# First MLP products begun before attention step 3 joins, first weight loads in halves, all weights loaded ahead of step 4

## The chip, the cores and the metric

The kernel runs on one core of a Trainium2 chip. The metric is the device time of one execution in microseconds (us). Executions more than 1.5% above the fastest of the same kernel are called slow and are left out of all comparisons. Each changed kernel ran beside the kernel before, on the same chip in the same rounds. Two changed kernels of different sets are compared by their medians, which is rougher. A ratio is the mean time of one kernel's fast runs over the mean of the other's of the same rounds, with a 95% interval, so it is not quite the ratio of the medians that stand beside it.

Engines in the profiles: PE multiplies matrices (PEld loads its weights), DVE, ACT and POOL are the vector, scalar and general engines, SP issues DMAs.

## The reference

A decayed linear attention in blocks of 64 tokens, then an MLP on its output:

```python
for b in range(12):                              # per batch and head
    intra = (qb @ kb.T * Dmask) @ vb
    inter = (qb * lam_pow) @ kv_state
    out[:, :, sl] = intra + inter
    kv_state = lam_block * kv_state + (kb * rev_pow).T @ vb
x = attention output as 3072 tokens x 512
return gelu_tanh(x @ w_in) @ w_out               # 512 -> 2048 -> 512
```

Inputs and output are float32; the kernel multiplies in float16 with float32 sums. q, k and v are 4 x 8 x 768 x 64, w_in and w_out are 4 MB each.

## The kernel before

The work is cut into 24 attention *steps* (256 tokens and half of the heads each). For one step: `load_step` (three DMAs of 256 KB), `prep` (scale and cast q, k, v), `stage_t` (transposes on PE, a copy to `qkT`), scores (`Sps`), causal mask (`PT`), products into two output banks (`OK`), a state update (`t` on DVE, `u` on POOL), and a copy into `xT`. Steps make *groups*: group 0 is steps 0 to 3 and has 512 tokens. When a group is in `xT`, its MLP is queued as *filler*: 16 products f (`mm1`: four matmuls of 512 columns and one gelu on ACT), then the second matrix product in parts of four matmuls (`mm2`). The schedule draws filler between the pieces of later steps. Some names that come up again: wi0 to wi3 and wo0 to wo3 are the 1 MB pieces of w_in and w_out; f counts the 16 blocks of 128 columns of w_in, c the four blocks of 128 rows that a product sums over; a *bank* is one of the six PSUM buffers of `ps_M`; t_2_1 is the `t` of `U(2)`.

```python
    pin(nc.sync.dma_start(out=lam_bc[:], in_=lam.unsqueeze(0).to_broadcast([P, H])))
    for s in range(4):
        load_step(s)
    for j in range(4):
        load_win(j)
    load_wout(0)
    load_wout(1)
    load_step(4)
    load_wout(2)
    load_wout(3)
    load_step(5)
    ...
    def cast_wout(j):                       # float32 piece j of w_out to float16
        for i in range(2):
            ...
            if i == 1 and j >= 2:
                pin(nc.scalar.activation(out=dst, in_=src, func=AF.Copy))
            else:
                pin(nc.gpsimd.tensor_copy(out=dst, in_=src))
    ...
        def mm1(f0):                        # one bank of the six in ps_M
            Hps = ps_M.tile([P, per, N], FP32, tag="M", name="Hps")
            ...                             # four matmuls
            pin(nc.scalar.activation(out=gT[:, f0 : f0 + per, :], in_=Hps[:],
                                     func=AF.Gelu_apprx_tanh))
    ...
    idle(12)                                # the head: steps 0 to 3
    prep(0)
    ...
    stage_t(3)
    idle(3)
    R(3, 2, split=True)
    idle(3)
    R(None, 3)                              # step 3 into xT; group 0 queued
    cast_win(0)
    U(2)                                    # t and u of the second block
    U(3)

    for j in range(1, 4):
        cast_win(j)
    for j in range(2):
        cast_wout(j)
    fill(17)                                # all 16 products and one mm2 part
    prep(4)
    cast_wout(2)
    cast_wout(3)
    stage_t(4)
    fill(3)
    R(4, None)
```

`pin` keeps instructions in program order on each engine. So `cast_wout(2)` stands on ACT behind all gelus of group 0.

## Time and profile before

| | before |
|---|---|
| median of 4 runs | 214.70 us (214.63 to 214.76) |
| span of the profiled execution | 213.5 us |
| PE busy | 205.1 us |
| last matmul's copy starts (end of PE's path) | 209.93 us |

The profiled execution took 215.29 us, 0.6 us above this median and outside the four runs. So a difference of up to some 0.6 us between this profile and another can be the execution's and not the kernel's.

### The profile page before, as it was taken

The numbers are of one execution on the slowest core, as the hardware profiler recorded it, in microseconds if no ns is written. First come the engines' busy times: TensorE is split into PE (matmuls) and PEld (weight loads), VectorE is DVE, ScalarE is ACT, GpSimd is POOL, SyncE is SP. The second block draws the span as 40 slices with busy tenths as digits, with TensorE's granted clock in tenths as the row PEclk, the third lists the DMA queues.
The fourth block names the chain that finished last, engine by engine and source line by source line (L and its number), as shares of the span: only waits on it lengthen the run. The fifth ranks groups of instructions, "written<-read, shape, count | busy, mean of one in ns | idle before, by whom it ended". The sixth has DMA issues, their size and how long they took to land.

```text
span 213.5 us, 5059 instructions
## 1 busy us (share of the span) xinstructions
PE 205.1 (96%) x2118; PEld 107.0 (50%) x2118; DVE 91.3 (43%) x179; ACT 94.2 (44%) x175; POOL 64.2 (30%) x82
## 2 busy tenths in 40 slices
PE   7879999999999999999999999999999999999993
PEld 2444444455875784444455455444455454444452
DVE  4887522478784523740464541363632241100121
ACT  2375774342672471477420577420576211475000
POOL 5493136454582333422421320432420110000000
PEclk9999999999999999999999999999999999999999
DMA  5999999999999999893675673615120012100112
GB/s 135 301 331 391 383 352 370 286 288 325 303 221 223 309 208 253 221 227 71 176 211 144 205 194 69 180 53 150 49 52 0 0 52 98 54 0 0 49 63 86
DMA packets 61879, 37.82 MB, mean 177 GB/s; under 512 B 17696, under 2 KB 54816, under 8 KB 61856
## 3 DMA queue, kind: packets, MB, share of 16 engines
q1 hardware_dynamic: 61696, 37.37, 63.4%
q8 instruction: 16, 0.26, 0.5%
q10 hardware_dynamic: 160, 0.13, 0.2%
q14 instruction: 7, 0.06, 0.1%
HBM read 27.27 MB, written 6.29 MB: 157 GB/s over the span
## 4 chain that ended last, share of the span: by engine, by line
PE 86%; DMA 7%; SPq 2%; ACT 2%; DVE 1%; issue 0%; ACTq 0%
PE Hps L376 38%; PE O2ps L387 34%; DMA k<-in_k_dram 7%; PE Sps L257 3%; PE OK L316 3%; PE OK L306 3%; SPq L67 2%; PE O2ps L407 2%; PE Tps L219 1%; PE OK L270 1%; ACT qkT L223 1%; ACT xT L324 1%; ACT qk L200 1%; DVE PT L291 0%; PE idle L432 0%
## 5 line engine op out<-in xcount | busy, mean ns | idle before, releaser
L376 PE MATMUL Hps<-xT,w_in 128*128 128x512 f16 (+1 forms) x448 | 86.0, 349 | 0.3 <-ACT xT L324 0.3
L387 PE MATMUL O2ps<-w_out,gT 128*128 128x512 f16 x368 | 82.9, 379 | 0.0
L378 ACT ACTIVATE gT<-Hps 128x512 f16<-128x512 f32 x96 | 57.3, 596 | 34.5 <-PE Hps L376 33.7
L376 PEld LDWEIGHTS <-w_in 128*128 128x128 f16 x448 | 43.3, 98 | 38.1 <-issue 0.6
L351 POOL TENSOR_TENSOR u<-t,lumask 128x256 f16<-128x256 f32 x40 | 27.9, 706 | 91.1 <-DVE t L347 64.2
L387 PEld LDWEIGHTS <-gT 128*128 128x128 f16 x368 | 35.3, 98 | 39.7
L291 DVE TENSOR_TENSOR PT<-Sps,mask 128x1024 f16<-128x1024 f32 (+1 forms) x25 | 29.4, 1180 | 45.2 <-PE Sps L257 45.2
L324 ACT ACTIVATE xT<-OK 128x256 f16<-128x256 f32 x48 | 18.3, 451 | 51.3 <-PE OK L316 39.5
L394 DVE COPY o<-O2ps 128x512 f32<-128x512 f32 x23 | 15.8, 690 | 52.6 <-PE O2ps L387 52.5
L201 POOL TENSOR_TENSOR v<-v,dv 128x512 f16<-128x512 f32 x24 | 25.9, 1081 | 4.7 <-DMA v<-in_v_dram 4.6
L195 DVE TENSOR_TENSOR qk<-q,dq 128x512 f16<-128x512 f32 x23 | 19.7, 859 | 6.9 <-DMA q<-in_q_dram 6.9
L200 ACT ACTIVATE qk<-k 128x512 f16<-128x512 f32 x24 | 15.0, 623 | 9.3 <-DMA k<-in_k_dram 9.3
L347 DVE SCALAR_TENSOR_TENSOR t<-t,lamu,OK 128x64 f32<-128x64 f32 x64 | 14.5, 274 | 2.4 <-PE OK L270 1.4
L432 PE MATMUL idle<-ones 128*128 128x512 f16 x30 | 10.2, 479 | 1.5 <-DVE ones L126 1.5
L257 PEld LDWEIGHTS <-qkT 64*64 64x64 f16 x384 | 6.1, 106 | 10.1 <-issue 6.8
L257 PE MATMUL Sps<-qkT 64*64 64x128 f16 x384 | 10.0, 222 | 0.9 <-ACT qkT L223 0.7
L103 POOL CAST w_out<-wo 128x1024 f16<-128x1024 f32 x6 | 6.6, 1113 | 12.4 <-DMA wo<-in_moe_w_out_dram 12.4
L306 PE MATMUL OK<-PT,v 64*64 64x128 f16 x384 | 10.2, 218 | 0.0
L316 PE MATMUL OK<-qkT,u 128*128 128x128 f16 x80 | 8.6, 222 | 0.0
L219 PE MATMUL Tps<-ident,qk 128*128 128x128 f16 x72 | 6.1, 221 | 2.2 <-DVE qk L195 1.0
L306 PEld LDWEIGHTS <-v 64*64 64x64 f16 x384 | 6.8, 108 | 0.9 <-issue 0.8
L219 PEld LDWEIGHTS <-qk 128*128 128x128 f16 x72 | 4.6, 99 | 5.0 <-DVE qk L195 1.8
(34 smaller groups left out, 54.4 us busy)
## 6 DMA issues: line engine op xcount, KB each, us to landing
q<-in_q_dram SPq DMA_DIRECT2D x24, 256.0 KB, 4.7
k<-in_k_dram SPq DMA_DIRECT2D x24, 256.0 KB, 4.9
v<-in_v_dram SPq DMA_DIRECT2D x24, 256.0 KB, 5.2
out_dram<-o SPq DMA_DIRECT2D x23, 256.0 KB, 2.7
wi<-in_moe_w_in_dram SPq DMA_DIRECT2D x4, 1024.0 KB, 11.4
wo<-in_moe_w_out_dram SPq DMA_DIRECT2D x4, 1024.0 KB, 9.4
qkT<-qk SPq DMA_TRANSPOSE x15, 3.4
out_dram<-o SPq DMA_DIRECT2D x1, 96.0 KB, 2.2
```

The source lines that it names most:

```text
L195: pin(q_eng.tensor_tensor(wide(tq), q32[:], decay(dq), ALU.mult))
L200: pin(nc.scalar.activation(out=wide(tk), in_=k32[:], func=AF.Copy))
L201: pin(nc.gpsimd.tensor_tensor(wide(tv[:]), v32[:], decay(dv), ALU.mult))
L257: pin(nc.tensor.matmul(Sps[half64(c), hl, hp, jk, :], o[half64(hl), 1, jk, hp, half64(c)], o[half64(hl), 0, :, hp, half64(c)], start=True, ...
L291: pin(nc.vector.tensor_tensor(dst.rearrange("p a c d -> p a (c d)"), src.rearrange("p a c d -> p a (c d)"), mask[:].unsqueeze(1).to_broadc ...
L306: pin(nc.tensor.matmul(OK[c][half64(hl), hp * P : hp * P + P], tv[half64(c), jk, 2 * hp + hl, :], PT[hp][half64(c), hl, jk, :], start=star ...
L324: pin(nc.scalar.activation(out=dst[:, :, c * P : (c + 1) * P].rearrange("p hp (t j) -> p hp j t", j=2), in_=OK[c][:, 0:256].rearrange("p ( ...
L351: pin(nc.gpsimd.tensor_tensor(bd[:], t[:].unsqueeze(2).to_broadcast([P, 2, 2, D]), lumask[:, 2 * half : 2 * half + 2, :].unsqueeze(3).to_b ...
L376: pin(nc.tensor.matmul(Hps[:, i, :], w_in16[:, c, f * P : (f + 1) * P], x[:, c, :], start=(c == 0), stop=(c == NC - 1)))
L378: pin(nc.scalar.activation(out=gT[:, f0 : f0 + per, :], in_=Hps[:], func=AF.Gelu_apprx_tanh))
L387: pin(nc.tensor.matmul(O2[tau][:], gT[:, f, tau * P : (tau + 1) * P], w_out16[:, f, :], start=(f == 0), stop=(f == NF - 1)))
L394: pin(nc.vector.tensor_copy(out=o32[:], in_=o2[:]))
```

## The change

The intent: the head spends 30 idle matmuls and several waits before the MLP can start. If products f=0 to 3 of group 0 begin with what is there (c=0,1 on all 512 columns, c=2,3 on the first 256, without step 3's heads and tokens) and step 3 joins later, PE has useful work sooner. For that the first w_in tiles must come sooner, hence the loads in halves, and the weights go ahead of step 4 in the queue of loads. Some smaller things are moved along with it. The core of the diff (cut: helpers that were split, and that DVE in place of ACT now copies step 3's `qkT`):

```diff
-    wst = ctx.enter_context(tc.tile_pool(name="wst", bufs=4))
+    wst = ctx.enter_context(tc.tile_pool(name="wst", bufs=6))
...
-    pin(nc.sync.dma_start(out=lam_bc[:], in_=lam.unsqueeze(0).to_broadcast([P, H])))
+    pin(nc.scalar.dma_start(out=lam_bc[:], in_=lam.unsqueeze(0).to_broadcast([P, H])))
     for s in range(4):
         load_step(s)
     for j in range(4):
-        load_win(j)
-    load_wout(0)
-    load_wout(1)
-    load_step(4)
-    load_wout(2)
-    load_wout(3)
-    load_step(5)
-    for s in range(6, 9):
+        load_win(j, 2 if j < 2 else 1)
+    for j in range(4):
+        load_wout(j)
+    for s in range(4, 9):
         load_step(s)
...
+        def mm1_begin(f):
+            first[f] = ps_M.tile([P, N], FP32, tag="M", name="Hps")
+            for c in range(NC):
+                w = N if c < 2 else SB
+                pin(nc.tensor.matmul(first[f][:, 0:w], ...))
+        def mm1_end(f):
+            for c in range(2, NC):
+                pin(nc.tensor.matmul(first[f][:, SB:N], ...))
+            pin(nc.scalar.activation(out=gT[:, f, :], in_=first.pop(f)[:],
+                                     func=AF.Gelu_apprx_tanh))
...
-    idle(12)
+    idle(11)
...
-    prep(3)
-    R(2, 1)
-    stage_t(3)
-    idle(3)
-    R(3, 2, split=True)
-    idle(3)
-    R(None, 3)
-    cast_win(0)
+    products(None, 2)
+    cast_win(0, 0, 128, 128)
+    cast_win(0, 128, 512, 128, on_act=True)
+    scores(3)
+    queue_group(0)
+    fill(1)
+    products(3, None)
+    update(3, 0)
+    causal(3)
+    fill(2)
+    products(None, 3)
+    fill(5)
+    cast_win(1, 0, 512, 128)
     U(2)
     U(3)

-    for j in range(1, 4):
+    for j in range(2, 4):
         cast_win(j)
-    for j in range(2):
+    for j in range(3):
         cast_wout(j)
-    fill(17)
+    fill(21)
+    cast_wout(3)
     prep(4)
-    cast_wout(2)
-    cast_wout(3)
     stage_t(4)
-    fill(3)
+    prep(5)
+    fill(2)
     R(4, None)
     U(4)
-    prep(5)
-    fill(4)
+    fill(1)
     stage_t(5)
     prep(6)
-    fill(2)
+    fill(1)
     R(5, 4)
```

More of the change, by code (lines that the diff above doesn't have):

```diff
@@ L74, with load_win @@
     wstage = {}
-    def load_win(j):
+    def load_win(j, halves=1):
+        w = 512 // halves
         t = wst.tile([P, NC, 512], FP32, tag="w32", name=f"wi32_{j}")
-        pin(nc.sync.dma_start(out=t[:], in_=moe_w_in[:, j * 512 : (j + 1) * 512].rearrange(
-            "(c p) f -> p c f", p=P)))
+        src = moe_w_in[:, j * 512 : (j + 1) * 512].rearrange("(c p) f -> p c f", p=P)
+        for i in range(0, 512, w):
+            pin(nc.sync.dma_start(out=t[:, :, i : i + w], in_=src[:, :, i : i + w]))
         wstage[("i", j)] = t
@@ L86, in load_wout, with cast_win @@
         wstage[("o", j)] = t
-    def cast_win(j):
-        t = wstage.pop(("i", j))
-        w = 128 if j == 0 else 256
-        for i in range(0, 512, w):
-            pin(nc.vector.tensor_copy(out=w_in16[:, :, j * 512 + i : j * 512 + i + w],
-                                      in_=t[:, :, i : i + w]))
+    def cast_win(j, lo=0, hi=512, w=256, on_act=False):
+        t = wstage[("i", j)]
+        for i in range(lo, hi, w):
+            dst = w_in16[:, :, j * 512 + i : j * 512 + i + w]
+            src = t[:, :, i : i + w]
+            if on_act:
+                pin(nc.scalar.activation(out=dst, in_=src, func=AF.Copy))
+            else:
+                pin(nc.vector.tensor_copy(out=dst, in_=src))
     def cast_wout(j):
@@ L180, in prep, with wide, decay, prep_v @@
     def prep(s):
-        half = s % 2
-        q32, k32, v32 = ld32.pop(s)
-        hs = slice(half * HH, (half + 1) * HH)
-        def wide(t):
-            return t.rearrange("p j h d -> p h j d")
-        def decay(t):
-            return t[:, hs, :].unsqueeze(3).to_broadcast([P, HH, 2, D])
+        prep_qk(s)
+        prep_v(s)
+    def wide(t):
+        return t.rearrange("p j h d -> p h j d")
+    def decay(t, s):
+        hs = halves[s % 2]
+        return t[:, hs, :].unsqueeze(3).to_broadcast([P, HH, 2, D])
+    def prep_v(s):
+        tv = a16p.tile([P, 2, HH, D], FP16, tag="v16", name=f"v16_{s}")
+        pin(nc.gpsimd.tensor_tensor(wide(tv[:]), ld32[s][2][:], decay(dv, s), ALU.mult))
+        a16[s] = a16[s] + (tv,)
+        if s >= 6:
+            load_ahead(s + 3)
+    def prep_qk(s):
+        q32, k32, _ = ld32[s]
         tqk = a16p.tile([P, 2, 2, HH, D], FP16, tag="qk16", name=f"qk16_{s}")
         tq, tk = tqk[:, 0], tqk[:, 1]
-        tv = a16p.tile([P, 2, HH, D], FP16, tag="v16", name=f"v16_{s}")
         q_eng = nc.gpsimd if s == 3 else nc.vector
-        pin(q_eng.tensor_tensor(wide(tq), q32[:], decay(dq), ALU.mult))
+        pin(q_eng.tensor_tensor(wide(tq), q32[:], decay(dq, s), ALU.mult))
         if s == 0:
@@ L200, in prep @@
         pin(nc.scalar.activation(out=wide(tk), in_=k32[:], func=AF.Copy))
-        pin(nc.gpsimd.tensor_tensor(wide(tv[:]), v32[:], decay(dv), ALU.mult))
-        a16[s] = (tq, tk, tv)
+        a16[s] = (tq, tk)
         if s >= FIRST_DMA_T:
@@ L207, in prep @@
             qkT[s] = o
-        if s >= 6:
-            load_ahead(s + 3)
     def stage_t(s):
@@ L213, in stage_t @@
             return
-        tq, tk, _ = a16[s]
+        tq, tk = a16[s][:2]
         Tps = ps_M.tile([P, 2, 2, 2, P], FP16, tag="M", name="Tps")
@@ L221, in stage_t @@
         o = qkp.tile([P, 2, 2, 2, P], FP16, tag="qkT", name=f"qkT_{s}")
-        if 1 <= s <= 3:
+        if 1 <= s <= 2:
             pin(nc.scalar.activation(out=o[:], in_=Tps[:], func=AF.Copy))
@@ L235, in half64, with scores, causal, products @@
         return slice(64 * i, 64 * i + 64)
-    def region(n, s, split=False):
+    Ss = {}
+    def scores(n):
+        o = qkT[n]
+        Sps = ps_S.tile([P, 2, 2, 2, P], FP32, tag="S", name="Sps")
+        for hp in range(2):
+            for jk in range(2):
+                for hl, c in TILES:
+                    pin(nc.tensor.matmul(
+                        Sps[half64(c), hl, hp, jk, :], o[half64(hl), 1, jk, hp, half64(c)],
+                        o[half64(hl), 0, :, hp, half64(c)], start=True, stop=True,
+                        skip_group_check=True))
+        Ss[n] = Sps
+    def causal(n):
+        t = ptp.tile([P, 2, 2, 2, P], FP16, tag="PT", name=f"PT_{n}")
+        pin(nc.vector.tensor_tensor(
+            t[:].rearrange("p a b c d -> p (a b) (c d)"),
+            Ss.pop(n)[:].rearrange("p a b c d -> p (a b) (c d)"),
+            mask[:].unsqueeze(1).to_broadcast([P, 4, 2 * P]), ALU.mult))
+        PTs[n] = t
+    def products(n, s):
         OK = [ps_M.tile([P, 512], FP32, tag="M", name=f"OK{c}") for c in range(2)]
@@ L248, in region @@
         if n is not None:
-            o = qkT[n]
             _, tk, tv = a16[n]
-            Sps = ps_S.tile([P, 2, 2, 2, P], FP32, tag="S", name="Sps")
-            def scores():
+            last = (n // 2) % NSB == NSB - 1
+            for jk in range(2):
                 for hp in range(2):
-                    for jk in range(2):
-                        for hl, c in TILES:
-                            pin(nc.tensor.matmul(
-                                Sps[half64(c), hl, hp, jk, :],
-                                o[half64(hl), 1, jk, hp, half64(c)],
-                                o[half64(hl), 0, :, hp, half64(c)], start=True, stop=True,
-                                skip_group_check=True))
@@ L263, in products @@
-            def products():
-                last = (n // 2) % NSB == NSB - 1
-                for jk in range(2):
-                    for hp in range(2):
-                        for c, hl in TILES:
-                            if c == 1 and last:
-                                continue
-                            pin(nc.tensor.matmul(
-                                OK[c][half64(hl), 256 + hp * D : 256 + hp * D + D],
-                                tk[half64(c), jk, 2 * hp + hl, :],
-                                tv[half64(c), jk, 2 * hp + hl, :],
-                                start=start(c, hl), stop=(jk == 1), skip_group_check=True))
-                Kps[n] = OK
@@ L277, in region @@
-            if split:
-                products()
-                update(n, 0)
-                scores()
-            else:
-                scores()
-                products()
-            PT = []
-            for hps in ([slice(0, 1), slice(1, 2)] if split else [slice(0, 2)]):
-                w = hps.stop - hps.start
-                t = ptp.tile([P, 2, w, 2, P], FP16, tag=f"PT{w}", name=f"PT_{n}_{hps.start}")
-                for src, dst in ([(Sps[:, :, hps.start], t[:, :, 0])] if split else
-                                 [(Sps[:].rearrange("p a b c d -> p (a b) c d"),
-                                   t[:].rearrange("p a b c d -> p (a b) c d"))]):
-                    pin(nc.vector.tensor_tensor(
-                        dst.rearrange("p a c d -> p a (c d)"),
-                        src.rearrange("p a c d -> p a (c d)"),
-                        mask[:].unsqueeze(1).to_broadcast([P, 2 * w, 2 * P]), ALU.mult))
-                PT += [t[:, :, i] for i in range(w)]
@@ L296, in region @@
-            PTs[n] = PT
+                    for c, hl in TILES:
+                        if c == 1 and last:
+                            continue
+                        pin(nc.tensor.matmul(
+                            OK[c][half64(hl), 256 + hp * D : 256 + hp * D + D],
+                            tk[half64(c), jk, 2 * hp + hl, :], tv[half64(c), jk, 2 * hp + hl, :],
+                            start=start(c, hl), stop=(jk == 1), skip_group_check=True))
+            Kps[n] = OK
         if s is None:
@@ L307, in region @@
                         OK[c][half64(hl), hp * P : hp * P + P], tv[half64(c), jk, 2 * hp + hl, :],
-                        PT[hp][half64(c), hl, jk, :], start=start(c, hl), stop=False,
+                        PT[half64(c), hl, hp, jk, :], start=start(c, hl), stop=False,
                         skip_group_check=True))
-        ins = ins_of.pop(s)
         for c in range(2):
-            u = ins[c]
-            if u is None:
+            if c == 0 and sbg % NSB == 0:
                 continue
+            u = us.pop((s, 0) if c else (s - 2, 1))
             for hp in range(2):
@@ L327, in region, with update @@
                 func=AF.Copy))
-    ins_of = {}
-    def update(s, c):
+    us = {}
+    def update(s, c, parts="tu"):
         sbg, half = divmod(s, 2)
         sb = sbg % NSB
-        if c == 0:
-            ins_of[s] = [state[half][1] if sb > 0 else None, None]
         if c == 1 and sb == NSB - 1:
@@ L339, in update @@
             return
-        OK = Kps[s] if c == 0 else Kps.pop(s)
-        K = OK[c][:, 256:384].rearrange("p (hp d) -> p hp d", hp=2)
-        t = ucp.tile([P, 2, D], FP32, tag=f"t{half}", name=f"t_{s}_{c}")
-        if sb == 0 and c == 0:
-            pin(nc.vector.tensor_copy(out=t[:], in_=K))
-        else:
-            for hp in range(2):
-                pin(nc.vector.scalar_tensor_tensor(
-                    t[:, hp, :], state[half][0][:, hp, :],
-                    lamu[:, 2 * half + hp : 2 * half + hp + 1], K[:, hp, :], ALU.mult, ALU.add))
-        bd = ubp.tile([P, 2, 2, D], FP16, tag=f"u{half}", name=f"u_{s}_{c}")
-        pin(nc.gpsimd.tensor_tensor(
-            bd[:], t[:].unsqueeze(2).to_broadcast([P, 2, 2, D]),
-            lumask[:, 2 * half : 2 * half + 2, :].unsqueeze(3).to_broadcast([P, 2, 2, D]),
-            ALU.mult))
-        state[half] = (t, bd)
-        if c == 0:
-            ins_of[s][1] = bd
+        if "t" in parts:
+            OK = Kps[s] if c == 0 else Kps.pop(s)
+            K = OK[c][:, 256:384].rearrange("p (hp d) -> p hp d", hp=2)
+            t = ucp.tile([P, 2, D], FP32, tag=f"t{half}", name=f"t_{s}_{c}")
+            if sb == 0 and c == 0:
+                pin(nc.vector.tensor_copy(out=t[:], in_=K))
+            else:
+                for hp in range(2):
+                    pin(nc.vector.scalar_tensor_tensor(
+                        t[:, hp, :], state[half][:, hp, :],
+                        lamu[:, 2 * half + hp : 2 * half + hp + 1], K[:, hp, :],
+                        ALU.mult, ALU.add))
+            state[half] = t
+        if "u" in parts:
+            u = ubp.tile([P, 2, 2, D], FP16, tag=f"u{half}", name=f"u_{s}_{c}")
+            pin(nc.gpsimd.tensor_tensor(
+                u[:], state[half][:].unsqueeze(2).to_broadcast([P, 2, 2, D]),
+                lumask[:, 2 * half : 2 * half + 2, :].unsqueeze(3).to_broadcast([P, 2, 2, D]),
+                ALU.mult))
+            us[(s, c)] = u
     groups = [[0, 1], [2], [3], [4, 5], [6, 7], [8, 9], [10, 11]]
@@ L367, in queue_group @@
         gT = gtp.tile([P, NF, N], FP16, tag="gT", name=f"gT_{g}")
-        x = xT.pop(g)
+        x = xT[g]
         per = 512 // N
@@ L412, in mm2_last @@
                     pin(eng.dma_start(out=dst[half64(j), lo:hi], in_=o32[half64(j), lo:hi]))
-        for f in range(0, NF, per):
+        first = {}
+        def mm1_begin(f):
+            first[f] = ps_M.tile([P, N], FP32, tag="M", name="Hps")
+            for c in range(NC):
+                w = N if c < 2 else SB
+                pin(nc.tensor.matmul(first[f][:, 0:w], w_in16[:, c, f * P : (f + 1) * P],
+                                     x[:, c, 0:w], start=(c == 0), stop=False,
+                                     skip_group_check=True))
+        def mm1_end(f):
+            for c in range(2, NC):
+                pin(nc.tensor.matmul(first[f][:, SB:N], w_in16[:, c, f * P : (f + 1) * P],
+                                     x[:, c, SB:N], start=False, stop=True,
+                                     skip_group_check=True))
+            pin(nc.scalar.activation(out=gT[:, f, :], in_=first.pop(f)[:],
+                                     func=AF.Gelu_apprx_tanh))
+        if g == 0:
+            for f in range(4):
+                filler.append(lambda f=f: mm1_begin(f))
+            for f in range(4):
+                filler.append(lambda f=f: mm1_end(f))
+        for f in range(4 if g == 0 else 0, NF, per):
             filler.append(lambda f=f: mm1(f))
@@ L436, in fill, with R @@
             filler.pop(0)()
-    def R(n, s, split=False):
-        region(n, s, split)
+    def R(n, s):
+        if n is not None:
+            scores(n)
+        products(n, s)
+        if n is not None:
+            causal(n)
         if s is not None and s % 2 == 1:
             g, i = group_of[s // 2]
-            if i == len(groups[g]) - 1:
+            if i == len(groups[g]) - 1 and g > 0:
                 queue_group(g)
-        if n is not None and not split:
+        if n is not None:
             update(n, 0)
@@ L468 @@
     idle(3)
-    U(1)
-    prep(3)
-    R(2, 1)
-    stage_t(3)
-    idle(3)
-    R(3, 2, split=True)
-    idle(3)
-    R(None, 3)
-    cast_win(0)
+    prep_qk(3)
+    scores(2)
+    products(2, 1)
+    update(2, 0)
+    prep_v(3)
+    causal(2)
+    stage_t(3)
+    idle(2)
+    U(1)
+    products(None, 2)
[11 more added lines that the diff above has]
+    cast_win(1, 0, 512, 128)
     U(2)
     U(3)
-    for j in range(1, 4):
+    for j in range(2, 4):
         cast_win(j)
-    for j in range(2):
+    for j in range(3):
         cast_wout(j)
-    fill(17)
+    fill(21)
+    cast_wout(3)
     prep(4)
-    cast_wout(2)
-    cast_wout(3)
     stage_t(4)
-    fill(3)
+    prep(5)
+    fill(2)
     R(4, None)
     U(4)
-    prep(5)
-    fill(4)
+    fill(1)
     stage_t(5)
     prep(6)
-    fill(2)
+    fill(1)
     R(5, 4)
     U(5)
-    fill(2)
+    fill(1)
     stage_t(6)
     prep(7)
-    fill(2)
+    fill(1)
     R(6, 5)
```

## The prediction

Some passages of the text are cut, and each cut is marked: statements of hardware that no trace or run shows, with them the reason given for "no cold clock" and the upper end of the range, 228.5 us, whose clock figure came from no trace. Three things were estimates, which the trace of before does not show: that PE falls to half speed after the wait, the chance of 0.85, and the 0.15 us for handovers. So are the shorter or absent slow stretches of rivals. The "first rise" is read from the idle matmuls, 0.43 us each against 0.216 later; the granted clock in the profile is 1.00 there as well.

> **What bounds the kernel now.** I began with the page's busy times and its chain that ended last, then the same chain in order of time, then the timelines of PE, ACT, DVE and POOL for the first 45 us.
>
> Busy times, from the page:
>
> ```profile
> PE 205.1 (96%) x2118; PEld 107.0 (50%) x2118; DVE 91.3 (43%) x179; ACT 94.2 (44%) x175; POOL 64.2 (30%) x82
> ...
> PE 86%; DMA 7%; SPq 2%; ACT 2%; DVE 1%; issue 0%; ACTq 0%
> ```
>
> PE is busy for 205.1 of 213.5 us, and the list of waits for PE from 60 us to the end is empty. So the order of filler work later on is worth nothing by itself; time can be won or lost only where PE waits or does idle work, which is in the first 45 us. The chain in order of time there (start, length, what):
>
> ```profile
> 18.51 0.65 PE idle L432 x3
> 19.16 0.36 PE OK L306 x16
> 19.52 0.23 PE OK L316 x2
> 19.78 0.77 ACT xT L324 x2
> 20.59 12.69 PE Hps L376 x58
> ```
>
> The head of the kernel is the attention of steps 0 to 3. PE keeps warm with 30 idle matmuls, and the MLP (Hps, "mm1") starts when step 3 is in xT: two matmuls at 19.69, the rest unbroken from 20.59. One product f is four matmuls of 512 columns, 0.864 us (16 gelus in ACT's timeline start 0.864 apart). So f=10, 38 matmuls of 0.216 after 20.59, begins at 28.8 us.
>
> The timelines of DVE and POOL give the weights' landings, as the end of the wait before each first cast:
>
> ```profile
> 21.84 1.52 DVE L92 CAST w_in<-wi 128x1024 f16<-128x1024 f32 x2 [0.51 <-DMA wi<-in_moe_w_in_dram]
> 24.51 1.30 DVE L92 CAST w_in<-wi 128x1024 f16<-128x1024 f32 x2 [1.15 <-DMA wi<-in_moe_w_in_dram]
> 27.23 1.30 DVE L92 CAST w_in<-wi 128x1024 f16<-128x1024 f32 x2 [1.42 <-DMA wi<-in_moe_w_in_dram]
> ```
>
> ```profile
> 29.98 2.02 POOL L103 CAST w_out<-wo 128x1024 f16<-128x1024 f32 x2 [7.77 <-DMA wo<-in_moe_w_out_dram]
> ```
>
> A 1 MB piece lands every 2.7 us: wi1, wi2, wi3, then wo0. ACT's timeline has the same for the later pieces:
>
> ```profile
> 34.17 0.60 ACT L378 ACTIVATE gT<-Hps 128x512 f16<-128x512 f32 x1 [0.27 <-PE Hps L376]
> 34.66 0.63 ACT L200 ACTIVATE qk<-k 128x512 f16<-128x512 f32 x1
> 38.22 1.06 ACT L101 ACTIVATE w_out<-wo 128x1024 f16<-128x1024 f32 x1 [2.93 <-DMA wo<-in_moe_w_out_dram]
> ```
>
> The reader should see the order: ACT casts its half of wo2 only after the last gelu of group 0, so its 2.93 us of waiting for the DMA costs nothing.
>
> [...] the 12 idle matmuls from 1.46 take 5.30 us, 0.43 each, against 0.216 later. [...] lam takes SP 0.40 us.
>
> **The change part by part.**
>
> *lam on ACT's queue, one idle matmul fewer in front.* q, k, v start about 0.45 us sooner on SP (0.74 instead of 1.20). lam still lands near 3.84, so q of step 0 is ready at 5.86 as now, but the first transposes no longer wait for the twelfth idle matmul (6.55). I give the head 0.35 us.
>
> *Head rearranged.* Idle matmuls go from 30 to 25. Four products begin with c=0,1 on all 512 columns and c=2,3 on 256: 24 matmuls in place of 16, but the same columns; 256-column ones run at 0.109 (16 in 1.75 us in the chain), so nothing is added. Walking durations of the old timelines through the new order: the causal mask of step 2 now stands behind t of step 2, which waits for the xT copy behind k of step 3 on ACT (near 14.8), so it ends near 16.4 (15.46 now). qkT of step 3 by DVE follows, then the first begun product near 18.0 against 19.69. A catch: the second output bank of step 3 is one that t_2_1 must have read, and t_2_1 stands on DVE behind four casts of wi1, the last two of which need its second half, near 21.9. So step 3 ends near 24, the four split products are whole near 25.3 (23.6 now), and the head has lost, not won. Whether that matters depends on the next part.
>
> *Weights ahead of step 4, and the casts moved.* In the built program, ACT's order after the four gelus of the split products is: **cast of the second half of wo2**, then the 12 gelus of f=4 to 15. In before this cast came after all gelus. It waits for wo2's DMA, which is behind 12 pieces of q, k, v, four MB of w_in and two of w_out. Landing of wo2: wi3 at 27.23, plus three pieces of 2.71 = 35.4; less 0.45 for the earlier start; plus about 0.6 for the 2 MB in halves, whose rows are 1 KB (estimate: in the windows 512 B rows of q, k, v move at 290 GB/s and 2 KB rows at 387, a straight line through the time per row gives 349 for 1 KB). So **35.5 us**.
>
> Meanwhile PE can do products only as far as there are banks: six, so f=4 to 9 (6 x 0.864 = 5.2), until about 30.5. f=10 needs the bank of f=4, so the gelu of f=4, so the cast. ACT: 35.5 + 1.06 (cast) + 0.60 (gelu) + 0.15 (handovers) = **37.3**. PE stands still for nearly 7 us, and where exactly the head ended no longer matters.
>
> *Step 4 to 7.* Loads of steps 4 and 5 are no later than now in total bytes, and PE will be late, so the 0.54 us wait for q of step 5 near 42.9 goes (with its neighbour, 0.6). But only one filler (0.86) now stands between the transposes of step 5 and its scores. DVE must do, after the second of two part-3 fillers: output copy 0.69, mask 1.22, t 0.46, copy 0.69, qkT 0.69, together about 3.65 with handovers; PE has 0.35 + 0.12 + 0.86 + 0.45 + 0.86 = 2.65 of work. A new wait of 1.0 us. The following ones come out even.
>
> *Clock.* After 7 us idle I expect half speed. In the trace the first rise took 1.46 to about 6.55, 5.1 us, so half of that, 2.55, is lost; with a chance of 0.85, 2.2.
>
> Sum: f=10 moves from 28.8 to 37.3, +8.5; -0.6; +1.0; +2.2: 214.7 + 11.1 = **225.8 us**, 5% slower. All else after f=10 is the same PE work.
>
> **The rivals.**
>
> *The intended gain.* Without the ACT wait, the head would win the idle matmuls and gaps between 15.2 and 20.6, at most some 1.5 us, and the 0.6 at 42.9: about 213, within 2%. For it: PE bound, and every microsecond of idle work counts. Against: the order on ACT leaves no way round the wait, and the landing cannot be before its bytes have moved: 3.15 MB by 13.5 us plus 7.34 MB at 387 GB/s is 32.5, less 0.45.
>
> *Landing at that bound.* Landings trail the bytes by about 1 MB now (wi3 at 27.23 when 8.4 MB had moved). Were wo2 to land at 32.0, PE would resume at 33.8: 214.7 + 5.0 - 0.6 + 1.0 and a shorter or no cold stretch, 220 to 222.
>
> *No cold clock.* [...] 223.5.
>
> *The head as the bound.* If ACT's wait were short, the t_2_1 wait would cost about 1.7 us: 216. It is hidden behind the later one.
>
> *DVE or POOL late.* POOL casts wo0 and wo1 by 34.4 and wo2's half with ACT; PE reaches them after 42. Hidden.
>
> **Range and chances.** The bound on bytes with a little cold gives 221.5[...]. Every variant that keeps the ACT wait is above 219.0, the 2% line. That leaves a misreading of the order or of the banks: 0.05 for the same, 0.01 faster, 0.94 slower.
>
> **What would show it.** In ACT's timeline of the changed kernel: four gelus until about 28, then idle for 7 us or more, ended by the DMA of wo, a 1.06 us cast near 35.5, then gelus 0.60 apart. In PE's: Hps until about 30.5, idle until about 37.3 with ACT gT as the releaser, then matmuls at 0.43 for some 5 us. A wait of 1 us on DVE's qkT at the scores of step 5. PE busy and the rest of the chain as now, only later. I am wrong if ACT's cast of wo2 is not idle before it, if wo2 lands before 32, or if PE's idle in the first 45 us does not grow.

## More of the kernel before

One more view is needed for comparison, the busy times by stretch. The columns are: stretch, its length, then busy us and number of instructions of PE, PEld, DVE, ACT and POOL, then the granted clock of PE, the busy share of the DMA engines, and GB/s. Kernel before:

```profile
core 0: us, PE busy (x) PEld busy (x) DVE busy (x) ACT busy (x) POOL busy (x), PEclk, DMA share, GB/s
...
30.00:37.00 7.00, 6.87 (x39) 3.29 (x37) 1.51 (x2) 3.96 (x7) 5.52 (x5) 1.00 1.09 351
37.00:42.00 5.00, 5.00 (x47) 2.29 (x44) 1.61 (x4) 1.82 (x2) 1.77 (x2) 1.00 1.05 297
```

PE is busy for 11.87 of these 12 us at a granted clock of 1.00; ACT has room (busy for 5.78).

## The result, and the profile after

| | before | after |
|---|---|---|
| median of 4 runs | 214.70 us (214.63 to 214.76) | 226.43 us (225.11 to 226.76) |
| ratio of fast runs | | 1.0535 [1.0493, 1.0577] |
| span of the profiled execution | 213.5 us | 224.7 us |
| last copy starts | 209.93 us | 220.72 us |

The changed kernel is correct and 5.3% slower. From the page of the changed kernel, the busy times and the chain by engine:

```profile
PE 206.9 (92%) x2121; PEld 107.9 (48%) x2121; DVE 87.8 (39%) x178; ACT 93.2 (41%) x177; POOL 65.3 (29%) x82
...
PE 79%; SPq 9%; DMA 6%; DVE 2%; ACT 1%; issue 1%
```

PE's busy time grew by 1.8 us (206.9 against 205.1) and the span by 11.2: most of the time is in PE's idleness, not in added work. The list of PE's waits (engine, tile, line, released by; us in total, times, longest) names it:

```profile
PE Hps L369 <- ACT gT L371: 6.1, 1, 6.1
PE OK L299 <- DVE t L339: 2.0, 1, 2.0
...
PE Sps L251 <- DVE qkT L231: 0.8, 1, 0.8
```

PE's timeline of the changed kernel shows where the first wait falls:

```profile
23.21 0.41 PE L299 MATMUL OK<-PT,v 64*64 64x128 f16 x15 [1.97 <-DVE t L339]
...
25.67 5.34 PE L369 MATMUL Hps<-xT,w_in 128*128 128x512 f16 x24
37.09 8.21 PE L369 MATMUL Hps<-xT,w_in 128*128 128x512 f16 x24 [6.08 <-ACT gT L371]
```

Six products, f=4 to 9, then a stop of 6.08 us until a gelu gives a bank back, then six more products that take 8.21 us for the same 24 matmuls. ACT's timeline shows what held the gelu:

```profile
25.21 2.07 ACT L423 ACTIVATE gT<-Hps 128x512 f16<-128x512 f32 x4 [0.57 <-PE Hps L420]
35.50 1.06 ACT L106 ACTIVATE w_out<-wo 128x1024 f16<-128x1024 f32 x1 [8.21 <-DMA wo<-in_moe_w_out_dram]
36.46 3.51 ACT L371 ACTIVATE gT<-Hps 128x512 f16<-128x512 f32 x7
```

Four gelus, 8.21 us of waiting for a DMA in front of a cast that nobody needs yet, then seven gelus in a row, six of them (f=4 to 9) on inputs that had been complete for up to ten microseconds. The stretches of the changed kernel show the clock (the same columns as before):

```profile
30.00:37.00 7.00, 1.01 (x5) 0.38 (x4) 0.00 (x0) 1.50 (x3) 5.08 (x5) 0.94 1.07 377
37.00:42.00 5.00, 4.91 (x12) 1.76 (x12) 0.71 (x1) 3.56 (x8) 2.08 (x2) 0.50 1.14 290
42.00:46.00 4.00, 4.00 (x18) 1.68 (x17) 0.00 (x0) 2.46 (x5) 1.04 (x1) 0.88 1.14 286
```

From 37 to 42 us PE is "busy" for 4.91 us but does 12 matmuls, at a granted clock of 0.50. Busy time alone would hide this.

### The profile page after: what moved, and what is told of

It is laid out like the page before. It is cut to its first block, busy times and chain, and to the rows that moved or that the text cites. A ratio compares the mean times of both kernels' runs of the same rounds, so it can differ in the third digit from the quotient of the medians.

```text
span 224.7 us, 5063 instructions
## 1 busy us (share of the span) xinstructions
PE 206.9 (92%) x2121; PEld 107.9 (48%) x2121; DVE 87.8 (39%) x178; ACT 93.2 (41%) x177; POOL 65.3 (29%) x82
## 3 DMA queue, kind: packets, MB, share of 16 engines
HBM read 27.27 MB, written 6.29 MB: 149 GB/s over the span
## 4 chain that ended last, share of the span: by engine, by line
PE 79%; SPq 9%; DMA 6%; DVE 2%; ACT 1%; issue 1%
PE Hps L369 34%; PE O2ps L380 34%; DMA wo<-in_moe_w_out_dram 6%; SPq L67 4%; SPq L81 3%; PE Sps L251 3%; PE OK L308 3%; PE OK L299 2%; PE O2ps L400 2%; SPq L86 1%; PE OK L285 1%; PE Tps L225 1%; DVE o L387 1%; DVE qkT L231 1%; DVE PT L259 1%
## 5 line engine op out<-in xcount | busy, mean ns | idle before, releaser
L371 ACT ACTIVATE gT<-Hps 128x512 f16<-128x512 f32 x92 | 54.2, 597 | 27.8 <-PE Hps L369 27.1
L369 PEld LDWEIGHTS <-w_in 128*128 128x128 f16 x432 | 42.5, 99 | 44.5 <-issue 9.9
L346 POOL TENSOR_TENSOR u<-t,lumask 128x256 f16<-128x256 f32 x40 | 28.7, 723 | 103.8 <-DVE t L339 80.7
L259 DVE TENSOR_TENSOR PT<-Sps,mask 128x1024 f16<-128x1024 f32 x24 | 29.3, 1222 | 51.4 <-PE Sps L251 51.3
L194 POOL TENSOR_TENSOR v<-v,dv 128x512 f16<-128x512 f32 x24 | 26.7, 1114 | 5.7 <-DMA v<-in_v_dram 3.9
L204 DVE TENSOR_TENSOR qk<-q,dq 128x512 f16<-128x512 f32 x23 | 18.0, 783 | 10.4 <-DMA q<-in_q_dram 10.4
L231 DVE COPY qkT<-Tps 128x1024 f16<-128x1024 f16 x7 | 4.8, 686 | 14.1 <-PE Tps L225 14.1
L449 PE MATMUL idle<-ones 128*128 128x512 f16 x25 | 8.3, 472 | 1.5 <-DVE ones L127 1.5
L108 POOL CAST w_out<-wo 128x1024 f16<-128x1024 f32 x6 | 6.1, 1038 | 8.8 <-DMA wo<-in_moe_w_out_dram 8.8
L285 PE MATMUL OK<-v,qk 64*64 64x64 f16 x320 | 7.1, 192 | 0.0
## 6 DMA issues: line engine op xcount, KB each, us to landing
wi<-in_moe_w_in_dram SPq DMA_DIRECT2D x2, 1024.0 KB, 11.1
```

The lines of the kernel that those rows point to most:

```text
L194: pin(nc.gpsimd.tensor_tensor(wide(tv[:]), ld32[s][2][:], decay(dv, s), ALU.mult))
L204: pin(q_eng.tensor_tensor(wide(tq), q32[:], decay(dq, s), ALU.mult))
L259: pin(nc.vector.tensor_tensor(t[:].rearrange("p a b c d -> p (a b) (c d)"), Ss.pop(n)[:].rearrange("p a b c d -> p (a b) (c d)"), mask[:]. ...
L346: pin(nc.gpsimd.tensor_tensor(u[:], state[half][:].unsqueeze(2).to_broadcast([P, 2, 2, D]), lumask[:, 2 * half : 2 * half + 2, :].unsqueez ...
L369: pin(nc.tensor.matmul(Hps[:, i, :], w_in16[:, c, f * P : (f + 1) * P], x[:, c, :], start=(c == 0), stop=(c == NC - 1)))
```

## The experiments

Twelve kernels ran, all correct. They aim at one of four questions: is it the cast's place on ACT, what does the clock cost, what does the head gain when the cast is out of the way, and what do the two loading edits do.

### The cast's place on ACT

**e1_cast_late**: the changed kernel with the third w_out piece cast after the gelus.

```diff
-    for j in range(3):
+    for j in range(2):
         cast_wout(j)
-    fill(21)
+    fill(12)
+    cast_wout(2)
+    fill(9)
     cast_wout(3)
```

> The changed kernel with the casts of wo2 moved behind the twelve products f=4 to 15, all else kept (loads ahead of step 4, new head). Theory (the ACT half of that cast, waiting for wo2's DMA in front of the gelus, stops PE; the clock falls on top): no long wait, f=10 starts straight after f=9 at about 30.9 us (28.8 before), no slow clock; 2.05 later from the head, 0.8 for the new wait at step 5, 1.15 less for waits of before that are gone: 216.4 us. Rival (loading all weights ahead of step 4 is what costs): the time stays above 221 us. Rival (the head's loss is the main part): also well above 220.

Measured: 218.98 us (218.52 to 219.14), ratio to before 1.0197 [1.0181, 1.0214]. PE's wait for ACT is gone from its list, and 7.5 us of the 11.7 with it. PE's timeline has f=4 to 15 without a stop:

```profile
27.08 10.81 PE L369 MATMUL Hps<-xT,w_in 128*128 128x512 f16 x48
```

But it is 2.6 us above what was expected. The stretch from 24 to 28 us gives the first part of the reason:

```profile
24.00:28.00 4.00, 4.00 (x19) 2.34 (x20) 1.53 (x3) 2.72 (x6) 0.79 (x2) 0.57 1.05 385
```

The clock was 0.57 there, after the 1.9 us wait for `t` in the head. That wait had been hidden behind the later one; uncovered, it cost its own length and a cold stretch. By the timeline, f=4 began 1.4 us later than in the changed kernel (27.08 against 25.67), 0.4 of it because `t` came later and the rest by the clock, and the 48 matmuls lost another 0.3: some 1.3 us of clock. The remaining 0.9 us is not in PE's path: between the profiles that path ends 3.4 us later (213.31 against 209.93), which is the expected 1.7 and this 1.7. The 0.9 is the time after the last copy (4.0 in place of 3.6 us) and the profile of before, which the expectation was built on and which is of an execution 0.6 us above its median.

**e2_cast_pool**: the order of the change kept, but POOL casts both halves of that piece, so ACT waits for nothing.

```diff
-            if i == 1 and j >= 2:
+            if i == 1 and j >= 3:
```

> The changed kernel with its order of casts kept, but both halves of wo2 cast by POOL, none by ACT. Theory: it is ACT's place in the queue that matters, not when wo2 is cast: POOL may wait for wo2 (35.5 to 37.6 us) without holding anything that PE needs before about 41 us, so 216.4 us as with the cast moved. Rival (the weights simply arrive too late for the MLP): 226 us as before the edit.

Measured: 217.77 us (217.58 to 218.73), ratio 1.0154 [1.0129, 1.0178]. A different mending of the same wait gives nearly the same result. The profiled execution is the slowest, and its clock in the same stretch was 0.62; the other three took 217.58 to 217.78 us, with mean clocks from 0.987 to 1.000, so the excess over 216.4 is not all clock. It is the engine's order that costs, not the cast or its load.

**e3_before_cast_early**: the kernel before with nothing but the cast moved ahead of the gelus.

```diff
-    for j in range(2):
+    for j in range(3):
         cast_wout(j)
     fill(17)
     prep(4)
-    cast_wout(2)
     cast_wout(3)
```

> The kernel before with one thing of the change alone: the casts of wo2 stand ahead of the first 17 fillers. Theory: ACT waits for wo2 until 38.2 us (there it lands behind step 4), f=10 starts near 40.0 instead of 28.8, the clock falls (3.0), the waits of 1.15 go: about 227.7 us, so the one line makes the whole loss and more. Rival (loss comes from the head, the halves or the order of loads): 214.7 us, unchanged.

Measured: 230.35 us (230.12 to 230.39), ratio 1.0728 [1.0712, 1.0744]. One moved line makes the kernel before slower than the whole change does. My size was short by 2.6 us, since I had used f=10 as the product that stops. Here the cast stands ahead of *all* gelus, so the six banks are f=0 to 5. ACT's and then PE's timeline of this kernel:

```profile
37.34 1.06 ACT L101 ACTIVATE w_out<-wo 128x1024 f16<-128x1024 f32 x1 [16.82 <-DMA wo<-in_moe_w_out_dram]
```

```profile
20.57 4.91 PE L376 MATMUL Hps<-xT,w_in 128*128 128x512 f16 x22 [0.31 <-ACT xT L324]
38.93 11.31 PE L376 MATMUL Hps<-xT,w_in 128*128 128x512 f16 x40 [13.45 <-ACT gT L378]
```

24 matmuls (two earlier, these 22), that is six products, then 13.45 us of nothing. The remaining 40 take 11.31 us, against 8.64 at 0.216 each: 2.7 us to the clock, which was granted at 0.50 from 37 to 42 us.

### The clock after the wait

**e4_keep_warm**: the changed kernel with 56 idle matmuls of 256 columns between f=9 and f=10, in the scores' banks, so that the wait is filled.

```diff
+    def idle_s(n):
+        t = ps_S.tile([P, 2, 2, 2, P], FP32, tag="S", name="idleS")
+        for _ in range(n):
+            pin(nc.tensor.matmul(t[:, 0, 0], ones[:, 0:P], ones[:, 0:256], start=True, stop=True))
...
-    fill(21)
+    fill(6)
+    idle_s(56)
+    fill(15)
```

> The changed kernel with 56 idle matmuls of 256 columns (6.1 us at full clock) in the scores' banks between f=9 and f=10, where PE waits. Theory: the wait keeps its length, but the clock does not fall, so the twenty-four matmuls behind it take 5.2 us and not 8.2: 223.4 us. Rival (slow matmuls have another cause, such as ACT's or DMA's traffic): 226.4 us, unchanged.

Measured: 224.10 us (223.72 to 225.08), ratio 1.0432 [1.0415, 1.045], 2.3 us less than the change. PE's timeline:

```profile
32.37 6.28 PE L454 MATMUL idleS<-ones 128*128 128x256 f16 x56
38.48 5.34 PE L369 MATMUL Hps<-xT,w_in 128*128 128x512 f16 x24
```

The same 24 matmuls take 5.34 us in place of 8.21, with a granted clock of 1.00 in place of 0.50 from 37 to 42 us: 2.9 us were the clock. The profiled execution is the slowest of the five: its earlier stretch, 24 to 28 us, had the clock at 0.57, so that the idle block began later than planned. The cast began at 36.00 there, the gelu that frees the bank ended at 37.57, and PE left the idle block at 38.48, 0.9 us later. The other four took 223.72 to 224.19 us.

### The head without the cast in the way

**e5_state_first**: the changed kernel with the state updates ahead of the casts of w_in's second tile, so that `t` no longer stands behind them. The later wait is kept.

```diff
     fill(5)
-    cast_win(1, 0, 512, 128)
     U(2)
     U(3)
+    cast_win(1, 0, 512, 128)
```

> The changed kernel, its cast of wo2 left where it is, with the state updates of steps 2 and 3 placed ahead of the casts of wi1 on DVE. Theory: the 2 us wait for t_2_1 goes and f=9 ends about 1.9 us sooner, but f=10 still waits for the gelu behind wo2's cast, at 37.1: 226.4 us, unchanged within 0.5 (the head is hidden). Rival (the head's loss adds to the time): 224.5 us.

Measured: 226.24 us (226.01 to 226.49), ratio 1.0533 [1.0519, 1.0548]: unchanged, as expected. The head's wait is gone and PE's wait for ACT has grown from 6.1 to 7.8 us, as its list of waits shows:

```profile
PE Hps L369 <- ACT gT L371: 7.8, 1, 7.8
```

What a wait costs can't be read from its length while a later one covers it.

**e6_late_and_state**: both edits, e1's and e5's, together.

> Both edits: casts of wo2 behind the products f=4 to 15, and the state updates of steps 2 and 3 ahead of the casts of wi1. The late-cast run alone was 219.0 and showed, beside the 2 us wait for t_2_1, the clock at 0.57 from 24 to 28 us. Theory (that wait costs 1.9 and, where it falls badly for the clock, some 1.5 more): 219.0 - 1.9 - 1.5 = 215.6, at best 214.5. Rival (the slow clock of 24 to 28 has another cause): 217.1.

Measured: 215.65 us (215.59 to 215.73), ratio 1.0041 [1.0029, 1.0053]. e5's edit alone is worth nothing and e1's alone 7.5 us; together they are worth 10.8. In its profile f=4 to 15 run in one stretch, PE's timeline:

```profile
24.00 10.52 PE L369 MATMUL Hps<-xT,w_in 128*128 128x512 f16 x48
34.36 7.93 PE L380 MATMUL O2ps<-w_out,gT 128*128 128x512 f16 x36
```

What is left of the change is 0.4% slower than before: its own aim, an earlier MLP, does not show in the time. (In the profiles the last copies start together, at 209.94 and 209.93 us, but that of before is of a slow execution.)

**e7_fill_step5**: e6 with one piece of filler moved to between step 5's transposes and its scores, where the change leaves a 0.8 us wait.

```diff
     cast_wout(2)
-    fill(9)
+    fill(8)
     cast_wout(3)
...
     stage_t(5)
     prep(6)
-    fill(1)
+    fill(2)
     R(5, 4)
```

> As the run with both edits, with one filler moved from before step 4 to between the transposes and the scores of step 5. Theory: the 0.8 us wait of the scores of step 5 for qkT falls to about 0.2: 0.6 us faster than the run with both edits. Rival (the wait moves on to step 6): the same time.

Measured: 215.56 us (215.25 to 216.85), ratio 1.0047 [1.0025, 1.0069]. The wait at step 5 is gone and one of 0.5 us has come at step 6. The rival was right: no gain.

**e8_masks_first**: e7 with the causal masks of steps 2 and 3 moved ahead of what stood before them on DVE, which takes away two waits of PE for `PT` in the head.

```diff
+    causal(2)
     update(2, 0)
     prep_v(3)
-    causal(2)
...
     scores(3)
+    causal(3)
...
     update(3, 0)
-    causal(3)
```

> As the run before, with the causal masks of steps 2 and 3 ahead of the state updates on DVE. Theory: the mask of step 2 no longer waits for the xT copy behind k of step 3 (15.47 to 14.3), step 3's mask no longer waits for the products of step 3 (19.7 to 18.0): f=4 starts about 22.5 to 23.0, sooner than the 23.6 of before, and 212.5 to 213.3 us, the first version ahead of the kernel before. Rival (landing of the weights or the casts on ACT bound the head): no faster than the run before it.

Measured: 215.42 us (214.24 to 215.98), ratio 1.0025 [1.0003, 1.0047]. A miss: expected was 212.5 to 213.3. The `PT` waits are gone, but in the profiled execution, the slowest of the six, lam was first used at 5.05 us (4.38 in the changed kernel, 3.90 in before), and the first transposes began 0.7 us later than in the changed kernel. That led to the last four kernels.

### The two loading edits, and the best version

These four ran on one chip, where the kernel before scattered more than elsewhere: median 214.75 us, ten of eleven runs fast, from 214.49 to 216.86. All ratios of this set are therefore wide.

**e9_lam_sp**: e8 with lam issued from SP again.

```diff
-    pin(nc.scalar.dma_start(out=lam_bc[:], in_=lam.unsqueeze(0).to_broadcast([P, H])))
+    pin(nc.sync.dma_start(out=lam_bc[:], in_=lam.unsqueeze(0).to_broadcast([P, H])))
```

> e8 with lam issued from SP again, as in the kernel before. Theory (lam's place on ACT's queue delays the head): lam lands near 3.9 as before, k0 near 5.45, and the head is 0.6 to 1 us sooner than in e8, so about 214.4 us against e8's 215.4. Rival (the late head of e8 was one execution's scatter, or is hidden before the first product): no change, 215.4, within 0.3.

Measured: median 214.79 us of six runs. The five fast ones are 213.98 to 214.93, ratio 0.9973 [0.9932, 1.0014]. The sixth, the profiled one, took 424.44 us with the clock recorded as 1.00 and matmuls nearly twice as long throughout (681 ns on average in `mm2`, 379 in the changed kernel's profile); it is slow, I can't explain it, and I take no time from it. The fast runs are 0.7 us under e8 by medians, as the theory has it in direction, but e8 ran on another chip and the intervals of the ratios overlap.

**e10_before_lam_act**: the kernel before with that line changed the other way, and nothing else.

> The kernel before with lam alone issued from ACT. My theory now: lam lands at 4.4 to 5.0 in place of 3.9 and k0 later too, so 0.2 to 0.4 us slower, 214.9 to 215.1. Rival (the prediction's: the loads behind lam on SP are 0.45 us earlier): 0.35 us faster, 214.4.

Measured: 215.42 us (215.34 to 215.92), ratio 1.002 [0.9984, 1.0055]. By medians 0.7 us slower, more than either expectation; by the ratio not shown. The landings are clear. Its POOL timeline, then ACT's:

```profile
4.36 2.02 POOL L152 TENSOR_TENSOR dq<-lam_bc,pos 128x4 f32<-128x4 f32 x2 [1.92 <-DMA lam_bc<-in_lam_dram]
```

```profile
6.04 0.63 ACT L200 ACTIVATE qk<-k 128x512 f16<-128x512 f32 x1 [3.35 <-DMA k<-in_k_dram]
```

In before these two begin at 3.90 and 5.47. With lam on ACT's queue they begin at 4.35 to 5.05 and 6.03 to 6.78 in all nine profiles (the change, e1, e2, e4 to e8 and this one; 5.05 and 6.78 are e8's); with lam on SP at 3.79 to 3.90 and 5.42 to 5.56 in the four fast ones (before, e3, e11, e12). It is not lam alone that is late: from 3 to 4 us all loads together moved at 154 to 216 GB/s in the nine and at 269 to 289 in the four, and SP's issue of step 1's k took 1.42 to 2.10 us against 0.51 to 0.59. The end of PE's path, 209.54 us against 209.93, says nothing about a loss, as the profile of before is of an execution 0.6 us above its median. So what the edit costs in time stays open; that it delays lam and the first k is shown.

**e11_fill_step6**: e9 with one more filler moved, to after the transposes of step 6.

```diff
-    fill(8)
+    fill(7)
     cast_wout(3)
...
     stage_t(6)
     prep(7)
-    fill(1)
+    fill(2)
     R(6, 5)
```

> e9 with one more transpose-free filler product moved from before the last cast to after the transposes of step 6. Theory (the wait of 0.5 to 0.7 us at step 6 is on PE's path): 213.8 us, 0.5 under e9. Rival (the wait moves on again, as from step 5 to step 6 in e7): as e9.

Measured: 215.12 us (214.51 to 215.7), ratio 1.0002 [0.9964, 1.004]. No gain over e9. Its list of PE's waits:

```profile
PE Hps L414 <- DVE w_in L98: 1.2, 1, 1.2
PE Tps L225 <- DVE qk L204: 1.2, 2, 0.7
...
PE Tps L225 <- ACT qk L209: 0.3, 1, 0.3
```

Two things are to be seen. The head now begins 1.2 us sooner than in e8 (first transposes at 5.82 against 7.07, and 6.37 in e6), but the first product then waits 1.2 us for the cast of the first w_in half: the loads bound it. And with less filler ahead of step 4, its transposes wait 0.68 us for q, which lands at 39.26 us here and at 33.76 in before, because all weights go first. The wait moved from step 6 to step 4. In this execution PE's path ended 0.8 us sooner than in before (last copy at 209.10 against 209.93, of which some 0.6 can be the slow execution of before), but the time from there to the end was 4.0 us in place of 3.6, and the six runs do not show a gain.

**e12_whole_loads**: e11 with the first two w_in tiles loaded whole.

```diff
-        load_win(j, 2 if j < 2 else 1)
+        load_win(j)
```

> e11 with the first two w_in tiles loaded whole, as in the kernel before. Theory (halves let the first cast start near 17.6 instead of 19.1, and 0.3 to 0.7 us of that reach the first products): 0.3 to 0.7 us slower than e11. Rival (the casts are bound by the last wi1 half either way): equal to e11 within 0.2.

Measured: 215.35 us (214.48 to 216.38), ratio 1.0011 [0.9961, 1.006]. The six runs fall in two sets: 214.48, 214.61 and 214.70 us with mean clocks of 0.998 to 1.000, and 216.00, 216.34 and 216.38 us with 0.992. The profiled one is of the second set, by stretches:

```profile
20.00:24.00 4.00, 3.99 (x31) 1.84 (x30) 2.77 (x11) 0.62 (x2) 3.07 (x3) 0.63 1.05 388
```

There the first product waited 1.8 us for its weights, and, by the mean clocks, half of the executions then lost the clock for a stretch; the other half did not, and are as fast as e11. By medians it is 0.2 us slower than e11, less than the 0.3 to 0.7 expected. The halves gain little directly, but they shorten the wait (1.2 us in e11, 1.8 here), and the clock from 20 to 24 us was 1.00 in e11's profile and 0.63 in this one. (Three against three runs: a pattern, not a rate.)

No version was shown to beat the kernel before. e9's fast runs come nearest, at 0.9973 with 1 inside the interval.

## Why the prediction was right

The prediction named one wait as the bound: f=10 behind a cast that ACT can't start before the third w_out piece lands. Its sum, term by term:

| term | predicted | measured | from |
|---|---|---|---|
| f=10 begins later | +8.5 | +8.3 | 28.8 to 37.09 |
| waits of steps 4 and 5 that go | -0.6 | -1.15 | 0.54, and two of 0.3 inside transposes |
| new wait at step 5 | +1.0 | +0.8 | list of waits |
| clock | +2.2 | +3.0 | 24 matmuls in 8.21 us, less 24 x 0.216 |
| sum | +11.1 | +10.95 | last copy: 220.72 - 209.93 = +10.8 |

The profiled spans differ by 11.2 us, of which 0.4 lie after PE's end; the medians differ by 11.7, since the profiled execution of before is 0.6 us above its median and that of the change 0.1. (From the last copy to the end it takes 3.6 us in the profiles of before and e3 and 3.9 to 4.1 in the other eleven fast ones; the cause is not known.)

Two slips of the working did not matter. The durations on DVE at step 5 add up to 3.75 us, not 3.65, so the new wait should have read 1.1. And the loads of step 4, with two more weight pieces ahead of them, were later: q was there at 39.14 us in place of 33.76, hidden because PE was later still.

**The wait.** The piece was predicted at 35.5 us and the cast began at 35.50. That the cast's place is the cause is shown from three sides: moved behind the gelus (e1) or to another engine (e2), the wait is gone, and put into the kernel before by itself (e3) it makes a wait of 13.5 us. That it is the bound is shown by e5: taking 2 us out of the head changes nothing. PE stood for 6.1, 7.8 and 13.5 us behind one waiting cast (the change, e5, e3) while gelus with complete inputs stood behind it: ACT took none of them ahead of the cast.

**How the landing came out.** Two terms went into it, 0.45 us earlier for lam's move and 0.6 later for the rows of 1 KB. The second has support: from 16 to 20 us the loads ran at 351 to 353 GB/s in three kernels with halves and at 386 to 388 in three with whole tiles (the estimate was 349 and 387), and the last w_in piece was cast at 27.44 with halves against 26.80 whole when lam is on ACT (the change, e10), at 27.27 against 26.47 when it is on SP (e11, e12). The first has none. SP issued the first load 0.46 us sooner, but the slow microsecond from 3 to 4 us (e10) took that back. And the base was late: the piece that was cast at 27.23 in before came at 26.51 in e3, whose loads are the same up to there, and at 26.47 in e12 with lam where before has it, against 26.80 in e10. In the nine fast profiles with halves the third w_out piece was there between 35.40 and 36.68 us. So the size was right and the exact 35.50 is luck.

**lam and the head: wrong.** I wrote that lam still lands near 3.84 and gave the head 0.35 us. It was used at 4.38, and the first k at 6.08, 0.6 us later than before. The first transposes came only 0.16 us sooner (6.39 against 6.55), and step 1's as before. It cost nothing in the sum because nothing in the head reached the end. The begun product's start (18.0 predicted, 18.23 measured), the whole split products (25.3, 25.67) and PE's stop (30.5, 31.0) were close.

**The clock: the fall right, the term small.** That the clock would fall was an estimate that no trace of before showed. I took half of the first rise and multiplied by a chance of 0.85. The chance should not have stood in a sum for a 6 to 13 us wait: the clock fell in every profile that has one and cost 3.0, 2.7 and 2.0 us there (the change, e3, e5). PE, back from these waits, ran at half clock for some 5.8, 5.1 and 3.8 us (estimates from the granted clock by stretches: 0.50, 0.50 and 0.56 from 37 to 42 us, 0.88, 0.74 and 1.00 from 42 to 46). Unweighted, 2.55 against 3.0 in the trace and 2.3 between medians (e4). Where a chance belongs is at waits near 2 us: the changed kernel waited 1.97 us at 21 to 23 us and kept its clock in that profile, while e1, e2 and e4 after the same wait fell to 0.57 to 0.62. Executions of one kernel differ in this too (e4's profiled one and its other four, e12's two sets). What decides it was not shown.

**The rivals.** "The head as the bound", at 216 us, was the outcome to expect with the ACT wait short. e1 and e2, which are that case, took 219.0 and 217.8: the 1.7 us wait was right (1.9 and 2.0). Missing were the clock, which fell after it in both profiles, and the new wait at step 5: with the prediction's own terms, 214.7 + 1.7 - 0.6 + 1.0 is 216.8. "The intended gain", about 213, was not reached by any version: with both orders mended (e6) the first products begin 1.3 us earlier (18.38 against 19.69), but the group's twelve whole products run until 34.36, against 33.97 in before for all sixteen. Nothing had been won by then, even with no stall left in between but the small ones of the head, and step 4's loads, late behind the weights, narrow the later slack. What the order of the loads costs by itself was not run.

## What to carry to other kernels

A cast put into the pinned stream of an engine waited for its load (8.21 us on ACT in the changed kernel), and the gelus behind it waited too, so that PE stood for 6.1 us: place it after the work whose results free buffers (e1), or on an engine that has nothing to give back (e2); count the banks to find how far PE gets meanwhile (six products in the change and in e3). Waits in sequence hid each other (e5's edit won nothing alone and 3.3 us after e1's), so mend the last one first and then measure the others, and expect some to move on rather than vanish (0.8 us at step 5 gave way to 0.5 at step 6 in e7). When a change moves work to an earlier place, ask what then arrives last there; in this kernel it was loads, which the change itself had put in a new order.
